# Attention over pooled queries and a multiplicative FFN on one core: each visit's order of work taken from a plan

## The chip, the cores and the metric

The kernel runs on one core of a Trainium2 chip. Its engines have queues of their own: PE multiplies matrices and writes the results into PSUM, DVE and ACT work elementwise and can read PSUM, POOL (GpSimd) works elementwise on SBUF, SP issues DMAs, as ACT and POOL also do. PSUM has eight banks of 128 partitions by 2 KB. The metric is the device time of one execution in microseconds (us); smaller is better.

## The reference

There are 8 batches of 8 heads, with 1152 keys of 64 elements. Neighbouring queries are averaged in pairs, so 576 queries are left for each head. Attention of these, its heads put side by side, is the input x of a feed-forward layer with 4608 tokens:

```python
q_pool = q.reshape(B, H, S // 2, 2, D).mean(axis=3)
scores = scale * np.matmul(q_pool, k.transpose(0, 1, 3, 2))
attn = softmax(scores)                      # over the 1152 keys
x = np.matmul(attn, v)                      # to (4608, 512): tokens by heads * 64
a = x @ w1                                  # (512, 1024)
b = x @ w2                                  # (512, 1024)
out = ((a * b) @ w3) @ w_out                # (1024, 1024), (1024, 512)
```

Nothing stands between w3 and w_out, so the kernel multiplies T = w3 @ w_out once, and then out = (a * b) @ T.

## The kernel before

Everything is unrolled and put on the engines' queues in the order in which the Python code names it; each engine works its queue in that order, and semaphores hold an instruction until its operands are there.

**Attention.** Two heads of one batch are a pair; there are 32 pairs. The loads (`load_kq`, `load_v`) bring K, Q and V in fp32, POOL casts K to fp16 and adds the query pairs (`cast_kq`), and casts V into a tile with a column of constants (`cast_v`), so that the row sums of the softmax come with the product. K and the queries of both heads, 14 blocks of 128 by 128, must be transposed into the tile `kqT`. For pair 0 that is done at the start by `first_loads`, `first_casts` and `first_turn`, for pairs 1 to 7 on PE by `transp_pe` (14 transposes into two PSUM banks, three DVE copies out), and from pair 8 on by a DMA on SP's queue (`transp`).

The scores of all pairs are one long row of columns, cut into 324 slots of 512 columns for each of two heads. `scores(s)` is one slot: matmuls of 64 rows for the two heads at once into a tile of two banks (tag `psc`, three such tiles, so six banks), then one exponential on ACT from it into a ring in SBUF (`ring`). `av_pair` multiplies 128 queries of a pair with V: 18 matmuls into a third of the bank `avb`; five such groups belong to a pair, 160 in all. `av_norm` divides by the row sums on DVE, and x is transposed into `xT`: on PE by `x_turn` and a DVE copy `x_copy` for the pairs below 8 and the last block of every pair, else by a DMA on SP's queue (`x_dma`). `av_step` does these for one group; the turn and copy of a group stand in the step of the next.

**FFN.** `moe_groups` yields the work of a chunk of 512 tokens as groups for PE, each with an evacuation: 8 times a projection with w1 (copied out by DVE) and one with w2 (multiplied with that copy by DVE), then four output groups of eight matmuls against T. `t_groups` yields what T needs: eight times a turn of w3's columns (eight transposes and a DVE copy to `w3T`) and a product of eight matmuls. `fill` takes the next group; it goes to the one bank of tag `mo`, or, if `scored` is true, to a bank of a `psc` tile. w3 comes in four quarters by POOL's queue (`w3_load`).

**The order.** A visit is three score slots and what stands behind them on PE until the next three; there are 108. The loop near the end of the kernel chooses it by counts: `credit` grows with each visit and decides between one AV group and two, and a visit gets two projections (or one group of two units) beside one AV group, and one beside two:

```python
n_av = 0 if not avail else 2 if credit >= (2.6 if two else 1.6) and avail > 1 else 1
credit -= n_av
n_f = 2 if n_av < 2 else 1
```

From visit 3 on T's groups are in the queue (`T_START`), one turn ahead of the products. After the last visit the remaining AV groups alternate with fills, then what is left of the FFN runs without attention. At the end one register is read and a general version of the kernel is skipped.

## Time and profile before

| what | value |
|---|---|
| median of three runs | 424.4 us (424.34 to 425.18) |
| the profiled execution | 425.14 us, its span 423.4 us |
| busy | PE 406.0, ACT 325.3, DVE 202.7, POOL 165.4 us |
| clock granted to PE in the record | 0.999 |
| first score matmul, first exponential | 7.46, 8.11 us |
| visit 18 starts, last visit starts | 69.51, 347.54 us |
| exponentials | 324, 1026 ns each in the record, 950 apart back to back |

A row of the timeline gives a start, the time from the first start to the last end, the engine, the line, what is written from what, the number of instructions (x8) and in brackets how long the engine was idle before and what it waited for. PEld is the loading of weights, which overlaps PE. SPq, ACTq and POOLq stand for the engines' issue of DMAs. Matmuls are pipelined and their ends are modelled, so starts are the surer number.

### The profile page before, as it was taken

The numbers are of one execution on the slowest core, as the hardware profiler recorded it, in microseconds if no ns is written. First come the engines' busy times: TensorE is split into PE (matmuls) and PEld (weight loads), VectorE is DVE, ScalarE is ACT, GpSimd is POOL, SyncE is SP. The second block draws the span as 40 slices with busy tenths as digits, with TensorE's granted clock in tenths as the row PEclk, the third lists the DMA queues.
The fourth block names the chain that finished last, engine by engine and source line by source line (L and its number), as shares of the span: only waits on it lengthen the run. The fifth ranks groups of instructions, "written<-read, shape, count | busy, mean of one in ns | idle before, by whom it ended". The sixth has DMA issues, their size and how long they took to land.

```text
span 423.4 us, 12643 instructions
## 1 busy us (share of the span) xinstructions
PE 406.0 (96%) x5273; PEld 249.6 (59%) x5273; DVE 202.7 (48%) x594; ACT 325.3 (77%) x357; POOL 165.4 (39%) x205
## 2 busy tenths in 40 slices
PE   3889999999999999999999999999999999999995
PEld 1457666666565656665666656666577766444442
DVE  2235554666355544554355534555355536624341
ACT  3968879889999998999889998999999991223231
POOL 4889866370571526323547314351643011000000
PEclk9999999999999999999999999999999999999999
DMA  8999999988494999969999959999994413020203
GB/s 269 256 306 280 289 299 326 261 218 257 144 285 100 264 279 267 258 154 274 299 183 338 268 131 231 254 293 310 280 175 103 58 44 84 12 101 0 99 2 105
DMA packets 90960, 86.34 MB, mean 204 GB/s; under 512 B 59664, under 2 KB 64272, under 8 KB 90896
## 3 DMA queue, kind: packets, MB, share of 16 engines
q1 hardware_dynamic: 81600, 59.52, 57.7%
q0 software_dynamic: 8720, 25.10, 21.1%
q8 instruction: 42, 0.69, 0.7%
q10 hardware_dynamic: 576, 0.85, 0.7%
q14 instruction: 22, 0.18, 0.2%
HBM read 67.11 MB, written 9.44 MB: 181 GB/s over the span
## 4 chain that ended last, share of the span: by engine, by line
PE 89%; DMA 4%; POOL 2%; DVE 2%; ACT 1%; issue 1%; SPq 0%; ACTq 0%; POOLq 0%
PE avb L316 21%; PE psc L291 18%; PE mot L409 16%; PE mo L409 14%; PE mo L447 10%; PE mot L447 5%; PE mo L388 3%; DMA w3c<-in_moe_w_dram 3%; DMA kst<-in_k_dram 1%; ACT ring L296 1%; PE ptk L233 1%; DVE kqT L235 1%; PE mot L388 0%; PE mol L465 0%; PE avb L349 0%
## 5 line engine op out<-in xcount | busy, mean ns | idle before, releaser
L296 ACT ACTIVATE ring<-psc 128x1024 f16<-128x1024 f32 x324 | 307.9, 1026 | 39.8 <-PE psc L291 38.5
L316 PEld LDWEIGHTS <-ring 128*128 128x128 f16 x2880 | 105.1, 98 | 35.3 <-issue 11.2
L316 PE MATMUL avb<-vaug,ring 128*128 128x65 f16 x2880 | 114.1, 193 | 1.5 <-DVE xT L358 1.5
L291 PE MATMUL psc<-kqT 64*128 64x512 f16 (+7 forms) x1152 | 96.0, 290 | 3.2 <-ACT ring L296 1.3
L205 POOL CAST kq<-kst 128x1152 f16<-128x1152 f32 x31 | 35.7, 1151 | 75.2 <-DMA kqT<-kq 46.1
L291 PEld LDWEIGHTS <-kqT 64*128 64x128 f16 x1152 | 45.5, 95 | 29.4 <-issue 6.3
L334 DVE RECIPROCAL rzall<-avb 128x2 f32<-128x2 f32 x160 | 26.3, 164 | 45.4 <-PE avb L316 29.9
L421 POOL DMA_DIRECT2D out_dram<-osb x21 | 11.7, 555 | 87.5 <-DVE rzall L334 87.5
L409 PEld LDWEIGHTS <-w2sb 128*128 128x128 f16 x320 | 28.3, 97 | 26.8 <-issue 2.9
L409 PEld LDWEIGHTS <-w1sb 128*128 128x128 f16 x320 | 28.0, 97 | 27.1 <-issue 3.5
L447 PEld LDWEIGHTS <-gT 128*128 128x128 f16 x280 | 25.4, 98 | 31.2 <-issue 4.0
L447 PE MATMUL mo<-T,gT 128*128 128x512 f16 x184 | 43.6, 380 | 0.0
L409 PE MATMUL mot<-xT,w2sb 128*128 128x512 f16 (+2 forms) x172 | 41.1, 364 | 0.0
L209 POOL TENSOR_TENSOR kq<-qst 128x512 f16<-128x512 f32 x31 | 39.4, 1271 | 1.7 <-DMA qst<-in_q_dram 1.7
L437 DVE TENSOR_TENSOR gT<-mot,asb 128x512 f16<-128x512 f32 x40 | 27.6, 692 | 23.6 <-PE mot L409 23.6
L218 POOL CAST vaug<-vst 128x1152 f16<-128x1152 f32 x32 | 36.6, 1143 | 4.0 <-DMA vst<-in_v_dram 3.7
L409 PE MATMUL mot<-xT,w1sb 128*128 128x512 f16 (+2 forms) x152 | 38.0, 373 | 0.0
L432 ACT COPY asb<-mot 128x512 f32<-128x512 f32 x20 | 11.7, 586 | 32.7 <-PE mot L409 32.7
L434 DVE COPY asb<-mo 128x512 f32<-128x512 f32 x35 | 24.2, 691 | 25.5 <-PE mo L409 25.5
L409 PE MATMUL mo<-xT,w1sb 128*128 128x512 f16 (+2 forms) x168 | 36.1, 344 | 0.0
L457 DVE TENSOR_SCALAR osb<-mo 128x512 f32<-128x512 f32 x23 | 15.9, 692 | 42.3 <-PE mo L447 42.3
L409 PE MATMUL mo<-xT,w2sb 128*128 128x512 f16 (+2 forms) x148 | 33.0, 351 | 0.0
(67 smaller groups left out, 269.9 us busy)
## 6 DMA issues: line engine op xcount, KB each, us to landing
vst<-in_v_dram SPq DMA_DIRECT2D x25, 576.0 KB, 5.0
kst<-in_k_dram SPq DMA_DIRECT2D x23, 576.0 KB, 5.8
qst<-in_q_dram SPq DMA_DIRECT2D x23, 512.0 KB, 6.8
out_dram<-osb POOLq DMA_DIRECT2D x21, 256.0 KB, 5.6
kst<-in_k_dram POOLq DMA_DIRECT2D x8, 576.0 KB, 9.5
qst<-in_q_dram POOLq DMA_DIRECT2D x8, 512.0 KB, 10.6
vst<-in_v_dram POOLq DMA_DIRECT2D x7, 576.0 KB, 6.4
out_dram<-osb SPq DMA_DIRECT2D x9, 256.0 KB, 2.1
```

The costliest lines, as they stand in the source:

```text
L205: nc.gpsimd.tensor_copy(out=kq16[:, 0:NJ].rearrange("p c u d -> p u c d"), in_=kst.rearrange("p u (c d) -> p u c d", d=D))
L209: eng.tensor_tensor(out=kq16[:, NJ:NJ + QM].rearrange("p c u d -> p u c d"), in0=qv[:, :, :, 0], in1=qv[:, :, :, 1], op=ALU.add)
L218: nc.gpsimd.tensor_copy(out=va[:, :, :, 0:D], in_=vs.pop(p).rearrange("p u (c d) -> p u c d", d=D))
L291: nc.tensor.matmul(psc[:, u, f - s * G:f - s * G + ln], kT2[u * 64:u * 64 + 64, jt, :], qpT[u * 64:u * 64 + 64, i0:i0 + ln], start=True, s ...
L296: nc.scalar.activation(out=ring[:, :, r0:r0 + G], in_=psc, func=AF.Exp, bias=0.0, scale=SCALE)
L316: nc.tensor.matmul(avb[:, o + u * E1:o + u * E1 + E1], ring[:, u, c0:c0 + 128], va[:, u, jt, :], start=(jt == 0 and u == 0), stop=(jt == N ...
L334: nc.vector.reciprocal(out=rzall[:, i, :], in_=av[:, :, D:E1].rearrange("p u o -> p (u o)"))
L409: nc.tensor.matmul(pw[:, d0:d0 + n], wt[:, mc, ft * 128:ft * 128 + 128], xT[:, mc, a:a + n], start=(mc == 0 and d0 == 0), stop=(mc == NC - ...
L434: nc.vector.tensor_copy(out=asb, in_=pa)
L437: nc.vector.tensor_tensor(out=gT[:, ft, :], in0=pb, in1=asb, op=ALU.mult)
L447: nc.tensor.matmul(po, gT[:, ft, tt:tt + 128], T16[:, ft, :], start=(ft == 0), stop=(ft == NF - 1))
L457: nc.vector.tensor_scalar_mul(out=osb, in0=po, scalar1=1.0 / (SCL * SCL))
```

## The change

A class `_Plan` keeps a reckoning of times: when PE is at which point, until when ACT and DVE are busy, and when each of the three `psc` tiles, the `mo` bank and the `av` bank come free, with fixed durations for each kind of work. For each visit `_Plan.visit` tries all orders of up to six items out of pair turns (P), up to three AV groups (A) and up to four fills (m for the `mo` bank, s for a scored bank), reckons three score slots behind each order, and takes the one with the least cost: time that PE loses, the distance to a time due (3.12 us for a visit), the wait of the AV bank, less a bonus for AV groups. The emission then follows that string. For the arrival of w3's quarters, of w_out and of pair 2 the plan has fixed times.

T's groups change their order and size: two turns of w3, then four half products of eight matmuls with 256 columns each. The tiles `w3T`, `gT` and `asb` are now taken when a group is emitted, since the queue is read four groups ahead; `near` is set there too.

The first pair: the second half of q is loaded by ACT's queue and the tail of q (64 KB) by SP's, ahead of the rest of K. The cast of K's first three blocks is POOL's, the query sums DVE's. `first_turn` uses one bank for each call: K's first three blocks go through the `mo` bank and are copied by ACT; the four query blocks go through the `av` bank, copied half by DVE and half by ACT; the last query block (`NB - 1`) follows behind slot 0; the other six blocks of K behind slot 2 as before.

In the changed kernel's order the visits 4 to 18 hold, behind their score slots (AV: AV group with its turn of x; half: half product):

```
4  AV, half, AV              9  half, pair 3, AV, half      14  AV, turn, turn, AV
5  AV, half, pair 2, AV      10 turn, AV, turn, half        15  half, pair 5, AV, half
6  half, half, AV            11 AV, half, AV                16  AV, half, AV
7  AV, turn, turn, AV        12 AV, pair 4, AV              17  AV, half, AV
8  half, half, AV            13 half, half, AV              18  projection, projection, AV
```

and before:

```
4  product, AV               9  AV, pair 3, turn, AV        14  AV, turn, AV
5  AV, pair 2, turn, AV      10 product, AV                 15  AV, pair 5, product
6  product, AV               11 turn, product, AV           16  product, AV
7  AV, turn, AV              12 AV, pair 4, turn, AV        17  AV, AV
8  product, AV               13 product, AV                 18  AV, projection, AV
```

The diff, without the lines that only pass on the changed tuples and tiles:

```diff
...
+class _Plan:
+    SWITCH, SLOT, AV, TURN, PAIR, SEEN = 0.09, 0.222, 0.553, 0.055, 0.76, 0.05
+    STEP = {0.5: 0.45, 1: 0.866, 2: 1.73}
+    def __init__(self, t):
+        self.t = t
+        self.act = self.mo = self.av = self.dve = 0.0
+        self.psc = [0.0, 0.0, 0.0]
+        self.k = 0
+        self.row = True
+    def _pe(self, row, free, took):
+        if row != self.row:
+            self.t += self.SWITCH
+            self.row = row
+        self.t = max(self.t, free) + took
+    def _psc(self):
+        self.k += 1
+        return (self.k - 1) % 3
+    def scores(self):
+        b = self._psc()
+        self._pe(True, self.psc[b] + self.SEEN, self.SLOT)
+        self.act = max(self.act, self.t + 0.21) + 0.953
+        self.psc[b] = self.act + 0.07
+    def fill(self, n, at, scored):
+        b = self._psc() if scored else None
+        self._pe(False, max(at, (self.psc[b] if scored else self.mo) + self.SEEN), self.STEP[n])
+        self.dve = max(self.dve, self.t + 0.2) + 0.69
+        if scored:
+            self.psc[b] = self.dve + 0.07
+        else:
+            self.mo = self.dve + 0.07
+    def av_group(self, turns):
+        self._pe(False, self.av + self.SEEN, self.AV + (self.TURN if turns else 0.0))
+        self.dve = max(self.dve, self.t + 0.2) + 0.49 + (0.21 if turns else 0.0)
+        self.av = self.dve + 0.02
+    def pair(self, at):
+        b = self._psc()
+        self._pe(False, max(at, self.psc[b] + self.SEEN), self.PAIR)
+        self.dve = max(self.dve, self.t + 0.1) + 0.9
+        self.psc[b] = self.dve + 0.07
+    def copy(self):
+        p = _Plan(self.t)
+        p.__dict__.update(self.__dict__)
+        p.psc = list(self.psc)
+        return p
+    def visit(self, due, turns, groups, pair_at, eager):
+        best = [None, None]
+        def end(p, seq, work, av):
+            q = p.copy()
+            for _ in range(3):
+                q.scores()
+            lost = q.t - self.t - work - 3 * self.SLOT
+            cost = lost + 0.2 * abs(p.t - due) + 0.3 * max(q.av + self.SEEN - q.t, 0.0)
+            cost -= eager * min(len(turns), 6) * av
+            if best[0] is None or cost < best[0] - 1e-9:
+                best[:] = [cost, seq]
+        def step(p, seq, work, av, f, pr):
+            if pr == len(pair_at):
+                end(p, seq, work, av)
+            if len(seq) > 5 or p.t > due + 0.5:
+                return
+            if pr < len(pair_at):
+                q = p.copy()
+                q.pair(pair_at[pr])
+                step(q, seq + "P", work + self.PAIR, av, f, pr + 1)
+            if av < min(len(turns), 3):
+                q = p.copy()
+                q.av_group(turns[av])
+                step(q, seq + "A", work + self.AV + (self.TURN if turns[av] else 0.0), av + 1, f, pr)
+            if f < min(len(groups), 4):
+                n, at = groups[f]
+                for b in (False, True):
+                    q = p.copy()
+                    q.fill(n, at, b)
+                    step(q, seq + "ms"[b], work + self.STEP[n], av, f + 1, pr)
+        step(self, "", 0.0, 0, 0, 0)
+        return best[1]
...
         qv = q[0, 0:2, 0:QM * 256].rearrange("u (p c) d -> p u (c d)", p=128)
         nc.scalar.dma_start(out=qst[:, 0, :], in_=qv[:, 0, :])
         nc.sync.dma_start(out=kst[:, :, 0:K0 * D], in_=kv[:, :, 0:K0 * D])
-        nc.scalar.dma_start(out=qtl, in_=q[0, 0:2, QM * 256:S].rearrange("u (p t) d -> p u (t d)", t=2))
-        nc.sync.dma_start(out=qst[:, 1, :], in_=qv[:, 1, :])
+        nc.scalar.dma_start(out=qst[:, 1, :], in_=qv[:, 1, :])
+        nc.sync.dma_start(out=qtl, in_=q[0, 0:2, QM * 256:S].rearrange("u (p t) d -> p u (t d)", t=2))
         nc.sync.dma_start(out=kst[:, :, K0 * D:], in_=kv[:, :, K0 * D:])
         kq[0] = (kst, qst, qtl)
...
     def first_casts():
-        kst, qst, qtl = kq.pop(0)
+        kst, qst, qtl = kq[0]
         kv = kst.rearrange("p u (c d) -> p u c d", d=D)
         qv = qst.rearrange("p u (c t d) -> p u c t d", t=2, d=D)
         o = kq16s[0].rearrange("p c u d -> p u c d")
-        nc.vector.tensor_copy(out=o[:, :, 0:K0], in_=kv[:, :, 0:K0])
-        nc.vector.tensor_tensor(out=o[:, 0, NJ:NJ + QM], in0=qv[:, 0, :, 0], in1=qv[:, 0, :, 1], op=ALU.add)
+        nc.gpsimd.tensor_copy(out=o[:, :, 0:K0], in_=kv[:, :, 0:K0])
+        for u in range(2):
+            nc.vector.tensor_tensor(out=o[:, u, NJ:NJ + QM], in0=qv[:, u, :, 0], in1=qv[:, u, :, 1], op=ALU.add)
         nc.gpsimd.tensor_tensor(out=kq16s[0][0:QT, NJ + QM], in0=qtl[:, :, 0:D], in1=qtl[:, :, D:2 * D], op=ALU.add)
-        nc.vector.tensor_tensor(out=o[:, 1, NJ:NJ + QM], in0=qv[:, 1, :, 0], in1=qv[:, 1, :, 1], op=ALU.add)
-        nc.gpsimd.tensor_copy(out=o[:, :, K0:NJ], in_=kv[:, :, K0:])
         kqT = att.tile([128, NB, 128], FP16, tag="kqT", bufs=3)
         pairs[0] = (*kq_views(kqT), kqT)
-    def first_turn(*parts):
+    def rest_casts():
+        kv = kq.pop(0)[0].rearrange("p u (c d) -> p u c d", d=D)
+        nc.gpsimd.tensor_copy(out=kq16s[0].rearrange("p c u d -> p u c d")[:, :, K0:NJ], in_=kv[:, :, K0:])
+    def first_turn(c0, c1, pt, *engs):
         kq16, kqT = kq16s[0], pairs[0][2]
-        pt = ps.tile([128, 512], FP32, tag="mo", bufs=1, name="ptf").bitcast(FP16)
-        o = 0
-        for c0, c1 in parts:
-            for c in range(c0, c1):
-                nc.tensor.transpose(pt[:, o + (c - c0) * 128:o + (c - c0) * 128 + 128],
-                                    kq16[:, c].rearrange("p u d -> p (u d)"), ident16)
-            o += (c1 - c0) * 128
-        o = 0
-        for c0, c1 in parts:
-            nc.vector.tensor_copy(out=kqT[:, c0:c1].rearrange("p c i -> p (c i)"), in_=pt[:, o:o + (c1 - c0) * 128])
-            o += (c1 - c0) * 128
+        for c in range(c0, c1):
+            nc.tensor.transpose(pt[:, (c - c0) * 128:(c - c0) * 128 + 128],
+                                kq16[:, c].rearrange("p u d -> p (u d)"), ident16)
+        w = (c1 - c0) // len(engs)
+        for n, eng in enumerate(engs):
+            o = n * w
+            eng(out=kqT[:, c0 + o:c0 + o + w].rearrange("p c i -> p (c i)"), in_=pt[:, o * 128:(o + w) * 128])
+    def turn_bank():
+        return ps.tile([128, 512], FP32, tag="mo", bufs=1, name="ptf").bitcast(FP16)
...
         w3T = {}
         def turn(ft):
-            w3T[ft] = msb.tile([128, NF, 128], FP16, tag="w3T", bufs=2, name="w3T")
             def go(pt):
+                w3T[ft] = msb.tile([128, NF, 128], FP16, tag="w3T", bufs=2, name="w3T")
                 ph = pt.bitcast(FP16)
                 for a in range(NF):
                     nc.tensor.transpose(ph[:, a * 128:a * 128 + 128],
                                         w3c[ft // 4][:, ft % 4, a * 128:a * 128 + 128], ident16)
-            return 1, go, lambda pt: nc.vector.tensor_copy(out=w3T[ft].rearrange("p a i -> p (a i)"),
-                                                           in_=pt.bitcast(FP16))
-        def mult(ft):
+            return 0.5, go, lambda pt: nc.vector.tensor_copy(out=w3T[ft].rearrange("p a i -> p (a i)"),
+                                                             in_=pt.bitcast(FP16)), W3_AT[ft // 2]
+        def mult(ft, n0):
             def go(pT):
                 for a in range(NF):
-                    nc.tensor.matmul(pT, w3T[ft][:, a, :], wosb[:, a, :], start=(a == 0), stop=(a == NF - 1))
-            return 2, go, lambda pT: nc.vector.tensor_copy(out=T16[:, ft, :], in_=pT)
-        yield turn(0)
-        for ft in range(NF):
-            if ft + 1 < NF:
-                yield turn(ft + 1)
-            yield mult(ft)
+                    nc.tensor.matmul(pT[:, 0:256], w3T[ft][:, a, :], wosb[:, a, n0:n0 + 256],
+                                     start=(a == 0), stop=(a == NF - 1))
+            return 1, go, lambda pT: nc.vector.tensor_copy(out=T16[:, ft, n0:n0 + 256], in_=pT[:, 0:256]), WO_AT
+        for ft in range(0, NF, 2):
+            yield turn(ft)
+            yield turn(ft + 1)
+            for n in range(4):
+                yield mult(ft + n // 2, n % 2 * 256)
...
-    def head():
-        while queue and not ahead:
+    def head(n=1):
+        while queue and len(ahead) < n:
             try:
                 ahead.append(next(queue[0]))
             except StopIteration:
                 queue.pop(0)
-        return ahead[0][0] if ahead else 0
+        return len(ahead)
     def fill(scored=False):
-        n = head()
-        if n:
-            _, go, put = ahead.pop()
-            pt = bank(scored) if put else None
-            go(pt)
-            if put:
-                put(pt)
-        return n
+        if not head():
+            return False
+        n, go, put, at = ahead.pop(0)
+        if not tail[0]:
+            plan.fill(n, at, scored)
+        pt = bank(scored) if put else None
+        go(pt)
+        if put:
+            put(pt)
+        return True
...
     first_casts()
+    rest_casts()
...
+    plan = _Plan(7.0)
+    PACE = 3.12
+    W3_AT, WO_AT, KQ_AT = (17.5, 28.0, 35.0, 44.0), 20.5, {2: 24.5}
...
-    seen = -1
-    credit = 0.0
-    vis = 0
-    while vis < NVIS or avn[0] < NU:
+    seen, due, started = -1, 0.0, False
+    for vis in range(NVIS):
         if vis == T_START:
             queue.append(t_groups())
+        due = max(due + PACE, plan.t + 2.6)
+        for s in range(vis * VS, vis * VS + VS):
+            pn = (s * G + G - 1) // FLAT
+            if pn != seen:
+                seen = pn
+                if pn == 0:
+                    first_turn(0, K0, turn_bank(), nc.scalar.copy)
+                    first_turn(NJ, NJ + QM, avb.bitcast(FP16), nc.vector.tensor_copy, nc.scalar.copy)
+                if NPE <= pn + 1 < NP:
+                    transp(pn + 1)
+                if 0 < pn < NP - 2:
+                    prepare(pn + 2)
+                elif pn + 2 == NP:
+                    cast_v(NP - 1)
+            scores(s)
+            plan.scores()
+            if s == 0:
+                first_turn(NB - 1, NB, turn_bank(), nc.vector.tensor_copy)
+        if vis == 0:
+            first_turn(K0, NJ, turn_bank(), nc.vector.tensor_copy)
+            prepare(2)
+        avail = NT5 * sum(1 for e in pair_end if e < vis) - avn[0]
+        turn = [p for p in range(1, NPE) if (p * FLAT // G) // VS - 1 == vis]
+        while ready:
+            started = True
+            queue.append(moe_groups(ready.pop(0)))
+        head(4)
+        for what in plan.visit(due, [on_pe(avn[0] + j - 1) for j in range(avail)], [(g[0], g[3]) for g in ahead],
+                               [KQ_AT.get(p, 0.0) for p in turn], 0.05 if started else 0.1):
+            if what == "P":
+                plan.pair(KQ_AT.get(turn[0], 0.0))
+                transp_pe(turn.pop(0))
+            elif what == "A":
+                av_step()
+                plan.av_group(on_pe(avn[0] - 2))
+            else:
+                fill(what == "s")
+    fill(True)
+    while avn[0] < NU:
+        av_step()
         while ready:
             queue.append(moe_groups(ready.pop(0)))
-        if vis < NVIS:
...
-        avail = NT5 * sum(1 for e in pair_end if e < vis) - avn[0]
-        turn = [p for p in range(1, NPE) if (p * FLAT // G) // VS - 1 == vis]
-        if vis >= NVIS:
-            fill(True)
-            while avn[0] < NU:
-                av_step()
-                fill(True)
-            break
-        credit = min(credit + NU / (NVIS - 5.0), float(avail)) if avail else 0.0
-        two = head() == 2
-        n_av = 0 if not avail else 2 if credit >= (2.6 if two else 1.6) and avail > 1 else 1
-        credit -= n_av
-        n_f = 2 if n_av < 2 else 1
-        if n_f == 2 and not turn:
-            if not two:
-                fill()
-            fill(not two)
-            if n_av:
-                av_step()
-        else:
-            if n_av:
-                av_step()
-            for p in turn:
-                transp_pe(p)
-            fill()
-            if n_av > 1:
-                av_step()
-        vis += 1
+        fill(True)
     tail[0] = True
     x_turn(NU - 1)
     x_copy(NU - 1)
```

## The prediction

> **What bounds the kernel now.** First the page's busy times and its slices, then the chain of what ended last.
>
> ```profile
> PE 406.0 (96%) x5273; PEld 249.6 (59%) x5273; DVE 202.7 (48%) x594; ACT 325.3 (77%) x357; POOL 165.4 (39%) x205
> ...
> PEclk9999999999999999999999999999999999999999
> ...
> PE 89%; DMA 4%; POOL 2%; DVE 2%; ACT 1%; issue 1%; SPq 0%; ACTq 0%; POOLq 0%
> ```
>
> PE ends the kernel, and the change leaves its work as it is: the same 324 score slots, 160 AV groups, 144 projections, 36 output groups, 64 transposes of w3, all in order on one queue. The time can then move only by what PE waits, so I need a list of waits. Busy time does not give it (matmul ends are modelled), but starts do: the distance from the first matmul of a group to the first of the next, less the shortest such distance of that kind, is the wait. The timeline of PE, undisturbed:
>
> ```profile
> 28.31 0.71 PE L316 MATMUL avb<-vaug,ring 128*128 128x65 f16 x18
> 28.86 0.22 PE L349 MATMUL avb<-ident,xbt 128*128 128x128 f16 x1
> 29.01 0.83 PE L291 MATMUL psc<-kqT 64*128 64x512 f16 x10
> 29.76 1.90 PE L388 MATMUL mo<-wosb,w3T 128*128 128x512 f16 x8
> 31.50 0.71 PE L316 MATMUL avb<-vaug,ring 128*128 128x65 f16 x18
> ```
>
> So an AV group is 0.55 us (28.86 - 28.31), its x transpose 0.15 with the change to scores, three slots 0.75, a T product 1.74. From the start of the w3 transposes at 33.59 to the AV at 34.47, below, 0.45 is work and the rest a wait; a pair turned on PE is 0.78, a projection 0.86 to 0.87, an output group 1.73. Measured against these, PE waits until 7.46 for its first score, then 13.3 us in visits 0 to 17 (up to 69.51), 6.1 us in visits 18 to 106, and next to nothing after the last score slots at 347.54. What can be won lies before 70 us.
>
> **Where the early waits are.** Visits 0 to 4 hold 7.3 us: ACT has nine exponentials back to back from 8.11 to 16.47 and PE has nothing else to do. The change brings no other work there. Then:
>
> ```profile
> 14.69 1.65 PE L233 MATMUL ptk<-ident,kq 128*128 128x128 f16 x14 [0.31 <-ACT ring L296]
> ...
> 24.89 0.95 PE L233 MATMUL ptk<-ident,kq 128*128 128x128 f16 x14
> 27.85 0.62 PE L379 MATMUL mo<-ident,w3c 128*128 128x128 f16 x8 [2.00 <-DMA w3c<-in_moe_w_dram]
> ...
> 34.47 0.72 PE L316 MATMUL avb<-vaug,ring 128*128 128x65 f16 x18 [0.27 <-DVE xT L358]
> ...
> 68.82 0.71 PE L316 MATMUL avb<-vaug,ring 128*128 128x65 f16 x18 [0.72 <-DVE xT L358]
> ```
>
> Visit 5 turns pair 2 at 24.89 and then stands 2.2 us for the second quarter of w3 (issued 16.88, landed 27.80). POOL's last cast for that pair ends at the same time:
>
> ```profile
> 24.39 0.45 POOL L211 TENSOR_TENSOR kq<-qtl 64x128 f16<-64x128 f32 x1
> ```
>
> Visits 6 to 17 hold 3.7 us in small waits: an AV or T product behind a w3 transpose (0.43, 0.36, 0.44 in visits 7, 11, 14), a second AV straight after the first (0.9, visit 17), T products behind the copies of pair and w3T (0.17, 0.17, 0.09), a pair waiting for its scored bank (0.20, 0.17), a late score slot (0.34, visit 15), and 0.4 in crumbs.
>
> **The change part by part.** The visits' contents of the changed kernel can be read from its instruction order.
>
> *The w3 turn of visit 5.* It moves to visit 7 as a pair of transposes; visit 5 becomes AV, half product, pair 2, AV. Visit 5 starts at 23.36 now; visit 4 gets some 0.4 shorter, its exponentials end near 22.7 and so free the last bank of visit 5 at about 22.9; with a slot, AV and half product behind that PE reaches the pair at about 24.7. But the cast ends at 24.84, so it starts at 24.9; then 0.78 + 0.55 + 0.15: visit 6 starts at 26.5 instead of 29.01, with 0.2 us more done (one AV more, one turn fewer). 2.7 us won. Its cover is the arrival of pair 2: each us by which that is later or earlier costs or gives one. The loads behind it keep their order on POOL's queue, with one cast of 384 columns added ahead of a cast that waits for its data until 7.68 anyway; I take 24.84, and 0.5 us either way for the range. The second quarter of w3 is then used near 31, the third (landed 34.8) near 40, the fourth (42.8) near 53. wosb, for which a POOL load waits until 20.38, is used at about 20.8.
>
> *Visits 6 to 17.* Two transposes together (0.9) cover the norm and the copy that the next AV waits for (0.69 after the matmuls), so the waits of 7, 11 and 14 go; the AV pair of visit 17 gets a half product between (0.86 against 0.93). A pair no longer shares a visit with a w3 turn, so its three copies (1.22 on DVE) do not stand ahead of w3T's. What is late next: three exponentials take 2.85, and these visits now hold 2.9 to 3.3 of PE work, so score slots will now and then wait 0.1; a pair right after an AV still waits 0.2. I leave 0.9 of 3.7: 2.8 won, between 1.8 and 3.3. DVE's eight more T copies are half as wide.
>
> *Half products.* 128 matmuls of 256 columns instead of 64 of 512. The nearest row is a projection cut in eight pieces: 0.87 against 0.86 in four, 2.5 ns a piece, so 64 more cost 0.16. The upper end, 0.5 us, is a weight load (98 ns) showing at times behind a 107 ns matmul.
>
> *The first pair.* K's first cast goes from DVE to POOL (about 0.1 slower), so the q sums don't wait behind it; the second half of q goes on ACT's queue, with 64 KB instead of 256 KB ahead of K's rest on SP's; q is copied in halves by DVE and ACT, and 128 columns of 640 wait until after slot 0. Both halves lie in one bank, and the instruction order shows ACT's copy waiting for DVE's, as here:
>
> ```profile
> 413.62 0.42 DVE L453 TENSOR_SCALAR osb<-mot 128x256 f32<-128x256 f32 x1 [0.96 <-PE mot L447]
> 414.08 0.38 ACT L454 ACTIVATE osb<-mot 128x256 f32<-128x256 f32 x1 [2.46 <-DVE osb L453]
> ```
>
> The halves follow each other, 414.08 after 413.62 + 0.42. So 0.25 + 0.38 take the place of 0.76, and the score starts at about 7.3, 0.2 earlier (ends: 0.5 earlier, 0.5 later if the q transfer is). Worth nothing: visit 5 waits for pair 2's cast either way. By the Trainium skill, PSUM — Partial Sum Buffer, "PSUM bank collisions raise a hardware error", ScalarE and VectorE must not touch one bank and the same partitions at once, two reads included; with that the halves can't overlap and the sum has nothing for it, without it 0.25 would be won ahead of the same cast. The pair of rows above agrees.
>
> *Visits 18 to 106.* Their work is the same by kind. 35 visits of two AVs and one projection (36 before) keep their waits of about 0.1. One visit holds two AVs alone (2.1 us of PE work, and ACT needs 2.85) and one a single output group (2.6): 0.8 and 0.25 lost. The waits before two pair turns (0.2 each) go, and some crumbs with the visits of three projections. Net 0.4 lost, between 0.6 won and 1.5 lost.
>
> *Sum.* -2.7 - 2.8 + 0.16 + 0.4 = -4.9 us. The profiled execution took 425.14 us (span 423.4 and 1.7 around), so 420.2 for one like it; it stands 0.74 above the median of 424.4, and 424.4 - 4.9 = **419.5 us**. Taking all good ends gives -2.7 - 0.5 - 3.3 - 0.6 = -7.1, all bad ones -2.2 - 1.8 + 0.5 + 1.5 = -2.0; these coming together is unlikely.
>
> **Rivals.**
> *The early visits gain little more than visit 5.* PE runs at half pace at first: pair 1's 14 transposes take 1.65 at 14.69, pair 2's 0.95 at 24.89, though the clock line shows 9 all along. The first eight w3 transposes take 0.83, the next eight 0.68, so the change comes near 19.3. Should it come one like stretch later, some 3.4 us of work takes twice its time, 1.7 lost; with 1.0 more of small waits kept, 422. For it: the start of the sequence is rearranged. Against it: visits 2 and 3 do the same work. By the Trainium skill, TensorE: Matmul & The Clock Gate, "What's actually happening", the clock opens after a busy window of about 3.4 us that runs free of the kernel; by that rule one window late is 1.7, as the rows give; no run here shows it late. Chance 0.2.
> *Slower: a pair's DMA transpose lands late.* From pair 8 on, kqT is turned by DMA from SP's queue, in order behind the transposes of x, which wait for AV norms.
>
> ```profile
> 131.33 1.19 SPq L326 DMA_TRANSPOSE xT<-xb  x1
> 132.62 1.54 SPq L225 DMA_TRANSPOSE kqT<-kq  x1
> ```
>
> This one is used at 140.1, 7.5 later. An x transpose stands directly ahead of 15 of 24 now, of 18 in the changed order. Landing took 4.0 to 12.0 us: a late issue with a long landing stalls all scores by up to 4.5. Two such lose the whole gain, three give 428; it decides from a landing over 7.2. Against it: every one that was issued this late landed in 4.0 to 6.2, the long ones were issued early. Chance 0.07.
> *The order is not what pays.* The visits with little PE work grow ACT gaps, and what is won early is given back later: 424.4. Chance 0.04; the counts above speak against it.
> *More than forecast.* Pair 2 arrives 0.5 earlier and the late visits gain 0.6: 418. Chance 0.08.
>
> **Numbers.** The forecast has the remaining 0.61, with a range of its own of 418.3 to 420.9. The 80% range adds most of the first rival and part of the good one: 418.0 to 422.5. This kernel's measurement tells 0.2% (0.85 us) from no change: faster 0.89 (forecast, better, first rival), same 0.04, slower 0.07.
>
> **What will show it.** Visit 18's first score near 65.5 (69.51 - 5.5 + 1.3 for work done sooner), the last three slots near 346.4 with 3.8 us less work behind them; no wait on w3c over 0.5; pair 2 still at 24.9; ACT's copy of q behind DVE's. Wrong would be: pair 2 later than 25.5, PE waiting on kqT from DMA, waits of visits 18 to 106 over 8 us in sum.

## The result, and the profile after

The changed kernel takes 423.3 us (median; 422.5 to 423.86), the kernel before, on the same chip in the same session, 425.18 us (424.34 to 427.45): a ratio of 0.9946, 95% interval 0.9925 to 0.9967. A second session gave 423.1 against 425.47 us, 0.9941 (0.9919 to 0.9963). By the ratio the change makes the kernel faster by 0.54%, 2.3 us (1.9 by the two medians); the prediction had 4.9. The time lies 3.8 above the forecast of 419.5 us. Of these, 0.8 come from the start of the sum: the kernel before had a median of 424.4 in its first three runs and of 425.2 to 425.9 later.

The page of the changed kernel, busy times, clock line and the chain by engine, shows PE bounding as before:

```profile
PE 406.1 (97%) x5337; PEld 252.5 (60%) x5337; DVE 205.9 (49%) x602; ACT 325.8 (77%) x358; POOL 165.7 (39%) x206
...
PEclk9999999999999999999999999999999999999998
...
PE 92%; DMA 3%; ACT 2%; DVE 1%; issue 0%; ACTq 0%; DVEq 0%
```

PE has 64 matmuls more, from the half products. The profiled execution took 422.73 us, with a span of 420.74, against 425.14 and 423.37 before. In its timeline around pair 2, start first, then duration:

```profile
24.11 1.04 PE L484 MATMUL mo<-wosb,w3T 128*128 128x256 f16 x8
24.98 0.94 PE L328 MATMUL ptk<-ident,kq 128*128 128x128 f16 x14
25.77 0.71 PE L413 MATMUL avb<-vaug,ring 128*128 128x65 f16 x18
26.32 0.22 PE L446 MATMUL avb<-ident,xbt 128*128 128x128 f16 x1
26.47 0.61 PE L388 MATMUL psc<-kqT 64*128 64x512 f16 x6
27.25 0.39 PE L388 MATMUL psc<-kqT 64*128 64x128 f16 x4 [0.17 <-DVE kqT L330]
...
31.54 0.61 PE L475 MATMUL mot<-ident,w3c 128*128 128x128 f16 x8
31.98 0.61 PE L475 MATMUL mo<-ident,w3c 128*128 128x128 f16 x8
32.42 0.71 PE L413 MATMUL avb<-vaug,ring 128*128 128x65 f16 x18
```

The second quarter of w3 is used at 31.54 without a wait, visit 6 starts at 26.47 instead of 29.01, and the AV group behind the pair of turns follows after 0.44. But the score slot at 27.25 now waits for a copy of pair 2.

The waits of PE, summed as in the prediction (the distance from a group's start to the next, less the shortest such distance of its kind: AV 0.55, projection 0.86, and so on), say where the time went. "Rest" is the span less all columns before it: work, and the end behind the last visit. Each row is one execution.

| execution | first score | visits 0-4 | 5 | 6-17 | 18-32 | 33-106 | rest | span |
|---|---|---|---|---|---|---|---|---|
| before | 7.46 | 7.26 | 2.39 | 3.68 | 1.32 | 4.80 | 396.46 | 423.37 |
| changed | 6.79 | 7.29 | 0.07 | 1.88 | 1.12 | 6.47 | 397.12 | 420.74 |
| changed, second session | 7.03 | 7.07 | 0.07 | 1.89 | 1.11 | 5.53 | 396.83 | 419.53 |

So 2.3 is won in visit 5, 1.8 in visits 6 to 17 and 0.2 in 18 to 32; 0.7 to 1.7 is given back in visits 33 to 106, and the rest grows by 0.4 to 0.7. The first score comes 0.4 to 0.7 earlier, but visit 3 does not (16.28 and 16.52 against 16.27), so this is no gain (see the first pair, below). These two executions lie 0.6 and 1.6 us below the medians of their kernel's runs, so the last half microsecond of the account is not to be trusted; visits 5 to 32 agree to 0.01.

The giving back has two places. In visit 62 two AV groups stand alone, and the second waits for the normalisation of the first:

```profile
205.06 0.83 PE L388 MATMUL psc<-kqT 64*128 64x384 f16 x10
205.82 0.72 PE L413 MATMUL avb<-vaug,ring 128*128 128x65 f16 x18
207.13 0.72 PE L413 MATMUL avb<-vaug,ring 128*128 128x65 f16 x18 [0.59 <-DVE xbt L439]
```

1.31 lie between the two groups instead of 0.55; visit 63 loses another 0.20, visit 75 (behind a lone output group) 0.32. In visit 81 something else happens:

```profile
256.94 7.50 SPq L423 DMA_TRANSPOSE xT<-xb  x2
...
264.53 2.44 SPq L320 DMA_TRANSPOSE kqT<-kq  x1
266.81 0.29 DVE L439 TENSOR_TENSOR xb<-avb,rzall 128x128 f16<-128x128 f32 x1 [0.95 <-DMA xT<-xb]
...
267.29 0.71 PE L413 MATMUL avb<-vaug,ring 128*128 128x65 f16 x18 [0.77 <-DVE xT L457]
```

DVE may not write the attention output `xb` of a new pair: its buffer, one of two, is still being read by a DMA transpose. The x copy for the next AV group stands behind that write on DVE, so PE waits 0.94. The kernel before has such a wait of DVE too (1.58 us at 272.97), but PE loses nothing by it.

### The profile page after: what moved, and what is told of

The parts are those of the page before. It is cut to its first block, busy times and chain, and to the rows that moved or that the text cites. A ratio compares the mean times of both kernels' runs of the same rounds, so it can differ in the third digit from the quotient of the medians.

```text
span 420.7 us, 12784 instructions
## 1 busy us (share of the span) xinstructions
PE 406.1 (97%) x5337; PEld 252.5 (60%) x5337; DVE 205.9 (49%) x602; ACT 325.8 (77%) x358; POOL 165.7 (39%) x206
## 4 chain that ended last, share of the span: by engine, by line
PE 92%; DMA 3%; ACT 2%; DVE 1%; issue 0%; ACTq 0%; DVEq 0%
PE avb L413 22%; PE psc L388 20%; PE mot L506 15%; PE mo L506 14%; PE mo L550 10%; PE mot L550 5%; PE mo L484 3%; DMA xT<-xb 2%; PE ptk L328 2%; ACT ring L393 1%; DMA qst<-in_q_dram 1%; PE mot L484 1%; PE mot L475 1%; DVE kqT L330 1%; PE mo L475 0%; PE mol L568 0%
## 5 line engine op out<-in xcount | busy, mean ns | idle before, releaser
L413 PEld LDWEIGHTS <-ring 128*128 128x128 f16 x2880 | 103.5, 98 | 33.4 <-issue 11.2
L550 PE MATMUL mo<-T,gT 128*128 128x512 f16 x192 | 45.5, 380 | 0.0
L506 PEld LDWEIGHTS <-w2sb 128*128 128x128 f16 x320 | 28.5, 97 | 26.5 <-issue 2.3
L506 PE MATMUL mot<-xT,w2sb 128*128 128x512 f16 (+2 forms) x164 | 40.1, 369 | 0.0
L506 PE MATMUL mo<-xT,w1sb 128*128 128x512 f16 (+2 forms) x172 | 39.2, 355 | 0.0
L535 DVE COPY asb<-mo 128x512 f32<-128x512 f32 x38 | 26.3, 692 | 23.5 <-PE mo L506 23.5
L506 PE MATMUL mot<-xT,w1sb 128*128 128x512 f16 (+2 forms) x148 | 34.9, 362 | 0.0
L506 PE MATMUL mo<-xT,w2sb 128*128 128x512 f16 (+2 forms) x156 | 34.0, 346 | 0.0
```

Of the source, the lines that this page charges most:

```text
L413: nc.tensor.matmul(avb[:, o + u * E1:o + u * E1 + E1], ring[:, u, c0:c0 + 128], va[:, u, jt, :], start=(jt == 0 and u == 0), stop=(jt == N ...
L506: nc.tensor.matmul(pw[:, d0:d0 + n], wt[:, mc, ft * 128:ft * 128 + 128], xT[:, mc, a:a + n], start=(mc == 0 and d0 == 0), stop=(mc == NC - ...
L535: nc.vector.tensor_copy(out=t["a"], in_=pa)
L550: nc.tensor.matmul(po, t["g"][:, ft, tt:tt + 128], T16[:, ft, :], start=(ft == 0), stop=(ft == NF - 1))
```

## Experiments

All kernels compute the whole reference. The kernel before, beside them on the same chip, had medians of 425.77, 425.88 and 425.47 us in the three sessions, in the order told here. The first session has the first four kernels, the second the next four, the third the last three.

| kernel | median us | ratio to before (95%) | 5 | 6-17 | 33-106 |
|---|---|---|---|---|---|
| late_counts | 422.98 | 0.992 (0.9889 to 0.995) | 0.07 | 1.89 | 5.01 |
| all_counts | 426.99 | 1.001 (0.998 to 1.004) | 0.44 | 3.65 | 8.50 |
| old_first | 423.07 | 0.9932 (0.9896 to 0.9968) | 0.08 | 2.22 | 5.83 |
| xb3 | 422.43 | 0.9908 (0.9876 to 0.994) | 0.07 | 1.89 | 5.69 |
| late_counts_xb3 | 422.55 | 0.9914 (0.9882 to 0.9945) | 1.47 | 1.88 | 6.02 |
| all_counts_xb3 | 423.64 | 0.9953 (0.993 to 0.9977) | 0.19 | 3.65 | 4.94 |
| held3_xb3 | 422.03 | 0.9902 (0.9863 to 0.9941) | 0.07 | 1.89 | 5.66 |
| t_old | 425.2 | 0.9989 (0.996 to 1.0019) | 0.18 | 4.25 | 6.67 |
| after2 (the change again) | 423.1 | 0.9941 (0.9919 to 0.9963) | 0.07 | 1.89 | 5.53 |
| whole | 425.24 | 0.9994 (0.9965 to 1.0022) | 0.18 | 2.98 | 8.49 |
| before_xb3 | 425.19 | 0.9988 (0.9961 to 1.0014) | 4.42 | 4.23 | 4.81 |

The last three columns are waits of PE by visits in the one profiled execution, in us.

### The plan, late and early

late_counts uses the old counting rule from visit 33 on, all_counts in every visit (`vis < 0`). Both keep the new groups of T and the new first pair.

```diff
-        for what in plan.visit(due, ...):
+        if vis < 33:
+            order = plan.visit(due, ...)
+        else:
+            n_av = 0 if not avail else 2 if credit >= (2.6 if two else 1.6) and avail > 1 else 1
+            ...
+        for what in order:
```

> Up to visit 32 as in the changed kernel, from visit 33 on the order by counts of the kernel before. PE's waits in visits 33 to 106 were 4.8 us before and are 6.5 in the changed kernel. Theory A (the plan's late orders cost this: a visit of two AVs alone, one of a single output group, visits of three projections): they fall to 4.8 to 5.1, and the time is 1.4 to 1.7 us below the changed kernel's, ratio to before about 0.991. Theory B (the late waits come with everything running some 4.8 us sooner, so that DMAs land late): they stay above 6 and the ratio stays at 0.994 to 0.995.

> No plan: every visit by the counts of the kernel before; T in pairs of turns and half products and the new first pair are kept. Theory A (the regrouping of T wins the early time, the plan little of it): visit 5 has no wait on w3, waits after the start up to visit 17 are 9 to 10.5 us (9.2 in the changed kernel, 13.3 before), those after it about 6 as before; ratio 0.990 to 0.993, at least as fast as the changed kernel. Theory B (the early time is won by the planned orders): waits up to visit 17 stay above 11.5 and the ratio is 0.996 or more.

With the old rule from visit 33 on, visits 33 to 106 wait 5.01: 0.5 less than the change's second execution, 1.5 less than its first. Part of the first difference is thus not the plan's. The time of late_counts can't be told from that of the change. Without the plan anywhere, visit 5 is still won (0.44): the new groups of T do that alone. Visits 6 to 17 are back at 3.65, so with the new groups the plan is worth 1.8 there; with the old groups it is worth nothing there (4.25 in t_old, below, against 3.68 before). By the same account the waits from the first score to the end of visit 17 come to about 12 us, and the ratio is 1.001, so of the two expectations theory B holds, but for visit 5. The late visits lost 3.7 more than before; in the timeline of all_counts:

```profile
273.62 0.29 DVE L439 TENSOR_TENSOR xb<-avb,rzall 128x128 f16<-128x128 f32 x1 [3.51 <-DMA xT<-xb]
...
274.10 0.71 PE L413 MATMUL avb<-vaug,ring 128*128 128x65 f16 x18 [1.53 <-DVE xT L457]
```

The wait for the buffer again, 3.51 on DVE here; PE lost 1.70 in front of this AV group and another 1.6 in the visit behind it, where it ran at half clock (last section).

### The third buffer

xb3, late_counts_xb3, all_counts_xb3 and before_xb3 are the changed kernel, the two above and the kernel before, each with one edit more:

```diff
-                xb5[p] = att.tile([128, QM, 2, D], FP16, tag="xb5", bufs=2, name="xb5")
+                xb5[p] = att.tile([128, QM, 2, D], FP16, tag="xb5", bufs=3, name="xb5")
```

> The changed kernel with three instead of two buffers for x on its way to SP's transpose (xb5). Theory A (visit 81's 0.94 us is DVE's write waiting for a buffer that SP's late transpose still reads): that wait goes, waits of visits 33 to 106 fall from 6.5 to 5.4 to 5.7, time 0.7 to 1.0 below. Theory B (the transpose itself is late and something else waits for it): the same time is lost at the next projection or score slot of that pair, and the sum stays.

> The changed kernel with the old counting rule from visit 33 on and a third buffer for the attention output that the DMA turns. Theory A (two separate losses behind visit 33: the plan's two poor visits, some 1.2 us, and a normalisation that waits until the DMA turn ahead has read its buffer, 0.4 to 0.9 us): PE's waits of visits 33 to 106 fall to 4.2 to 4.9 us (5.01 with the old rule alone, 5.69 with the third buffer alone, 6.47 in the changed kernel, 4.80 before), the wait of the normalisation on the DMA is gone from DVE, and the time is 0.988 to 0.991 of the kernel before. Rival B (the late loss is one thing that both edits remove, so together they give no more than either): waits 5.0 to 5.7 us and 0.991 to 0.993.

> No plan in any visit (the old counting rule throughout), T as pairs of turns with half products and the new first pair kept, and a third buffer for the attention output that the DMA turns. Theory A (without the plan the early waits of visits 6 to 17 stay, and the loss of visits 33 to 106 was the buffer alone): visit 5 waits 0.4 us, visits 6 to 17 some 3.6 us as before, visits 33 to 106 4.6 to 5.2 instead of 8.5, and the time is 0.993 to 0.996 of the kernel before: what the new groups of T win alone. Rival B (the old rule with the new groups of T is bad for the late visits for its own order): visits 33 to 106 stay over 6.5 us and the time within 0.998 to 1.002.

> The kernel before with a third buffer for the attention output that the DMA turns, and nothing else. Theory A (the normalisation waits for that buffer in the kernel before as well, but PE feels only 0.4 us of it, in visit 79): visits 33 to 106 wait 4.3 to 4.6 us against 4.80, no wait of the normalisation on the DMA is left, and the time is 0.997 to 1.000 of the kernel before. Rival B (the third buffer's 0.0038 in the changed kernel came from elsewhere, as from other addresses or other DMAs): the time is 0.994 to 0.997 here too, with visits 33 to 106 unchanged.

DVE waits for the DMA of `xb` in six of the eight profiles with two buffers (0.6 to 3.5 us) and in none of the five with three. all_counts falls from 1.001 to 0.9953, as expected, with 4.94 instead of 8.50. xb3 gives 0.9908, its interval overlapping that of the change, so a gain by the third buffer under the plan is not shown; the second execution of the change, with two buffers, had no wait for it either.

Two expectations failed. late_counts_xb3 should have waited 4.2 to 4.9 behind visit 33 and waited 6.02. Two events are in it that its sister does not have: 0.72 in visit 95 in the middle of a projection, where the record names no cause ("issue"), and 0.38 in visit 93. Without them it is 4.92, hardly better than late_counts: the profiles fit two separate losses, that of the plan's late orders and the buffer's, the second not in every execution; the times do not show them apart. The same profile shows an event that the prediction had priced:

```profile
25.79 1.26 POOL L304 TENSOR_TENSOR kq<-qst 128x512 f16<-128x512 f32 x1 [1.55 <-DMA qst<-in_q_dram]
27.02 0.44 POOL L306 TENSOR_TENSOR kq<-qtl 64x128 f16<-64x128 f32 x1
...
27.52 0.95 PE L328 MATMUL ptk<-ident,kq 128*128 128x128 f16 x14 [1.23 <-POOL kq L306]
```

Pair 2's queries landed late, its cast ended 2.7 later than in the changed kernel's profile, and visit 5 waited 1.47.

before_xb3 should have shown 4.3 to 4.6 behind visit 33. The wait of DVE is gone, but PE's waits stay at 4.81, and so does the 0.4 of visit 79 that had been put down to it (a score slot behind an exponential). So in the kernel before the short buffer costs nothing.

### The projections held back

held3_xb3 lets the FFN start a chunk when three AV groups instead of five are still ahead of it, so that visit 62 gets a projection between its two AV groups (third buffer as above).

```diff
-    HELD = 5
+    HELD = 3
```

> The plan in all visits, with three AV groups held back ahead of the FFN instead of five, and a third buffer as in the run before. The order changes in visit 62, which then holds a projection between its two AV groups. Theory A (the 0.96 us of visits 62 and 63 is an AV group that waits for the normalisation of the one straight ahead of it): this wait goes, visits 33 to 106 wait 4.5 to 5.0 us against 5.69 with the third buffer alone, 0.989 to 0.991 of the kernel before. Rival B (the projections were held back because their x would not be there yet): a projection waits for the DMA of x by 0.5 us or more at the chunk borders, and visits 33 to 106 stay at 5.5 to 7.

The wait of 0.76 in visit 62 is gone and that of 0.20 in visit 63 smaller, as theory A has it. The sum is still 5.66, as with five (5.69). The waits of 0.26 and 0.38 in visits 54 and 75 stand in xb3 as well (0.26 and 0.33); new are 0.21 and 0.30 in visits 87 and 100 and 0.1 to 0.2 more in each of visits 78, 80, 82, 91 and 106. Theory A was right on the place and wrong on the sum. The time, 0.9902, is the lowest of all kernels, with an interval that overlaps that of xb3.

### The groups of T

t_old has T's old groups under the plan (one turn, then a whole product). whole has pairs of turns, but whole products (its edit, with the lines of the 512-column product left out):

```diff
...
-            for n in range(4):
-                yield mult(ft + n // 2, n % 2 * 256)
+            for n in range(2):
+                yield mult(ft + n)
```

> The changed kernel with T's old groups: one turn of w3 ahead of each whole product of 512 columns; the plan and the new first pair stay. Theory A (the plan alone moves the second turn out of visit 5, since it knows when the second quarter of w3 lands; the regrouping matters for the small waits only): visit 5 waits under 0.4 us, visits 6 to 17 wait 2.2 to 3.7 us against 1.88, and visits 18 to 106 7.0 to 8.0, so that the time is 0.995 to 1.000 of the kernel before. Rival B (the regrouping is what moves the turn of w3 behind visit 5): PE stands over 1.5 us for w3's second quarter in visit 5 or 6, and the time is 0.999 to 1.004. Half products cost 0.2 us in the sum by distance of starts (0.88 a half against 1.724 a whole), and this goes in both theories.

> The changed kernel with two turns of w3 ahead of two whole products instead of four half products; plan and first pair stay. Theory A (the pairs of turns cover the copies that an AV group waits for, 1.3 us in three visits of the kernel with the old groups of T; the halves fill the visits, worth about 1 us, at 0.2 to 0.3 us of PE time): no wait of 0.4 us behind a turn of w3 is left, visits 6 to 17 wait 2.3 to 3.2 us against 1.88 and 4.25, and the time is 0.995 to 0.999 of the kernel before. Rival B (the halves are what the plan needs): visits 6 to 17 stay at 3.8 us or more, and the time is 0.998 to 1.002. Rival C (the halves are worth nothing): 2.0 us or less, and 0.992 to 0.995.

Visit 5 is won in both (0.18). So either part, plan or groups, moves the use of w3's second quarter behind its arrival; the prediction credited the groups. Visits 6 to 17 are 4.25 with single turns, 2.98 with pairs, 1.88 with half products. With single turns the AV group behind each still waits, here in t_old (0.88 from the start of the turn, 0.45 of it work):

```profile
32.54 0.61 PE L475 MATMUL mo<-ident,w3c 128*128 128x128 f16 x8
...
33.42 0.71 PE L413 MATMUL avb<-vaug,ring 128*128 128x65 f16 x18 [0.27 <-DVE xT L457]
```

Three such waits of 0.43 are the 1.27 between 4.25 and 2.98, so the pairs do what was said; the halves bring another 1.1, most of it in score slots (in whole six of them wait 0.25 to 0.46, in the change two wait 0.33). t_old's 6 to 17 lie outside the 2.2 to 3.7 expected. In whole, 1.95 of the 8.49 in the late visits is the buffer (visit 54), 0.70 an "issue" wait as above (visit 96); the 5.84 left are near the 5.53 of the change. Its time, 0.9994, lies above the 0.995 to 0.999 expected: of the 2.1 us between its median and the change's, visits 6 to 17 explain 1.1. The rest fits its late visits, but whole was not run with a third buffer.

### The first pair

old_first has the loads, casts and the turn of the first pair as in the kernel before.

```diff
...
-                    first_turn(0, K0, turn_bank(), nc.scalar.copy)
-                    first_turn(NJ, NJ + QM, avb.bitcast(FP16), nc.vector.tensor_copy, nc.scalar.copy)
+                    first_turn((0, K0), (NJ, NB))
...
```

> The changed kernel with the loads, casts and turns of the first pair as before. Theory A (the earlier first score is given back at once: slot 1 waits for the late query block, slot 3 for the rest of K): first score at 7.4 to 7.5 instead of 6.8, slot 3 and visit 3 start where they do in the changed kernel (10.4 and 16.3), time within 0.3 us of it. Theory B (the 0.67 us is kept): visit 3 and the end come 0.5 to 0.7 later.

The first score is 0.81 later (7.60 against 6.79), but visit 3 starts at 16.40 against 16.28; the ratio, 0.9932, can't be told from that of the change. Nothing was won. In the changed kernel's timeline:

```profile
6.04 0.29 DVE L373 COPY kqT<-avb 128x256 f16<-128x256 f16 x1 [0.70 <-PE avb L368]
6.37 0.37 ACT L373 COPY kqT<-avb 128x256 f16<-128x256 f16 x1 [0.56 <-DVE kqT L373]
6.79 0.61 PE L388 MATMUL psc<-kqT 64*128 64x512 f16 x2 [0.79 <-ACT kqT L373]
...
7.94 1.03 PE L388 MATMUL psc<-kqT 64*128 64x64 f16 x8 [0.32 <-DVE kqT L373]
...
10.38 1.30 PE L388 MATMUL psc<-kqT 64*128 64x320 f16 x10 [0.38 <-DVE kqT L373]
```

Slot 1 waits at 7.94 for the query block that was put off, and a later slot at 10.38 for K's rest (10.34 before). What the first slot gains ends there: from the first score to visit 3 the changed kernel takes 9.49 us, old_first 8.80 and the kernel before 8.81.

### The change again

> The changed kernel once more, beside the same runs of the kernel before as the next two, for what one execution can tell. Theory A (its waits are set by its order, the waits for a DMA and the start vary from one execution to the next): visit 62 waits 0.7 to 0.8 us again and visits 6 to 17 wait 1.8 to 1.95; the normalisation's wait for the DMA turn of the output ahead of visit 81 lies anywhere from 0 to 1.5 us on PE, and start and visits 0 to 4 together between 14.0 and 15.3 us; the time is 0.993 to 0.997 of the kernel before. Rival B (that wait is fixed by the order as well): 0.9 to 1.0 us in visit 81 again.

Visit 62 waits 0.76 again, visits 6 to 17 wait 1.89, start and visits 0 to 4 take 14.10. In visit 81 nothing waits this time, although SP issues the two transposes of `xb` at 256.96 as against 256.94 in the first execution: the issue is the same, so the wait depends on when they land. Rival B falls.

## Why the prediction was right or wrong

**Bound and direction: right.** PE bounds before and after, and the gain is in waits. In the changed kernel's profile none of the three signs of a wrong forecast came: pair 2 is not later than 25.5, PE waits for no kqT from DMA, the waits of visits 18 to 106 are 7.6 us, under 8. They were set too wide: the forecast was missed without any of them. Visit 6 starts on time (26.47 against 26.5), visit 18 at 66.21 against 65.5, the last three slots at 348.28 (347.36 in the second session) against 346.4.

**Visit 5: the number right, its cover in part by luck.** Pair 2 starts at 24.98 (forecast 24.9), visit 6 at 26.47 (26.5). But POOL's cast does not hold it:

```profile
24.32 0.44 POOL L306 TENSOR_TENSOR kq<-qtl 64x128 f16<-64x128 f32 x1
```

The cast ends at 24.76, and PE starts the pair 0.87 after the half product ahead of it (24.11 to 24.98), the shortest such distance. PE came 0.3 later than the 24.7 reckoned, and so the two ends met by chance. That a late pair 2 would cost shows in late_counts_xb3, where the cast ends 2.7 later: visit 5 waits 1.47 there, the rest being covered, since visit 5 itself starts 1.1 later (23.87). Of the 2.7 forecast, 2.39 was there to win as a wait, so some 0.4 is work moved between visits; and the plan alone would have won it as well.

**Visits 6 to 17: the step that failed.** "I leave 0.9 of 3.7: 2.8 won, between 1.8 and 3.3": 1.88 are left, 1.8 won, the bad end. The named waits of 7, 11 and 14 and of visit 17 went, the pairs alone taking 1.27. Mis-sized is "what is late next", which had 0.9 for all: score slots wait 0.33 in visits 6 and 13 each (the first for copies of pair 2), the turns of w3 wait 0.12 and 0.18 behind an AV group, pair 4 waits 0.16, and 0.8 are crumbs. Where a score slot waits for an exponential, the table's 950 ns from one to the next is too long: the nine from 8.11 take 8.36 us, 0.92 apart, and the plan reckons with 0.953.

**Visits 18 to 106: sized right by its order, one wait not seen.** "Net 0.4 lost, between 0.6 won and 1.5 lost" was 0.5 lost in the second execution and 1.47 in the first; the difference is 0.94 of the buffer. The 0.8 for two AV groups alone is the 0.76 of visit 62. The slower rival looked at SP's queue, but at the wrong user: no kqT was late; the DMA transpose of x, in the same queue behind loads and before kqT, held a buffer that DVE writes.

**Half products: 0.16 forecast.** Two halves in a row start 0.88 apart (33.91 to 34.79) against 0.87 for half of a whole: 16 of them make about 0.16. The rest of the account grew by 0.4 to 0.7, though; t_old and whole, with whole products, show 0.3 to 0.4 of it too, so the halves do not explain it all. The new first pair is a likely part: it adds 0.68 between the first score and visit 3 (9.49 against 8.81), with one turn and its slot more there, and the account counts part of this as work. How much was not tried.

**First pair: the value right, the cause wrong.** The first score came at 6.66 to 7.35 in the ten profiles of kernels with the new first pair (7.3 forecast), and it is worth nothing. But not because visit 5 waits for pair 2: the gain ends in visits 0 to 3. Visit 5 starts 0.6 earlier (22.73 against 23.36), but that is won in visits 3 and 4, where 0.25 us of work less is done and less is waited. ACT's copy starts at 6.37, after DVE's 6.04 + 0.29, like the pair of rows in the trace of before. The Trainium skill, PSUM — Partial Sum Buffer, "PSUM bank collisions raise a hardware error", has it that ScalarE and VectorE must not touch one bank and the same partitions at once; the trace agrees.

**The rivals.** The first came nearest by what it wins (2.4), by a mechanism that did not happen in this profile: pair 1 takes 1.65 and pair 2 0.94 after as before, and of the first two turns of w3 the second is fast already. In other profiles that change of pace comes later; the second turn first in the changed kernel, then in late_counts, which has the same order up to there:

```profile
19.07 0.64 PE L475 MATMUL mo<-ident,w3c 128*128 128x128 f16 x8
```

```profile
19.63 1.06 PE L475 MATMUL mo<-ident,w3c 128*128 128x128 f16 x8
```

From visit 3 to visit 5 late_counts takes 6.91 us, the changed kernel 6.45 and 6.23 in its two executions. The second turn takes 1.06 in five of the 13 profiles, old_first with its old first pair among them, so this looks like scatter of about half a microsecond and not like the doing of the change. Of "what is won early is given back later" a part came true: 0.7 to 1.7 of the 4.3 won up to visit 32.

**The sum.** For one execution like the profiled one 420.2 was forecast, and it took 422.73, 2.5 more: 1.0 from visits 6 to 17, 1.1 from the late visits, 0.4 from visit 5 and 0.5 from the rest, less 0.6 at the first score; 0.2 lies outside the span. (The 0.6 and the 0.5 belong together in part, as the 0.68 up to visit 3 shows.) The bad ends of all terms together would have made 2.0 won and 422.4 us; with the 0.8 by which the kernel before was slower later, 423.2. So what put 423.3 outside 418.0 to 422.5 was the two mis-sized terms and a base taken from three runs, after the judgement that the bad ends "coming together is unlikely".

## What to carry to other kernels

Where a queue is re-ordered, look at every buffer that a slow DMA still reads, not only at what the DMA delivers: here a third buffer of `xb` is the cheapest edit seen: all_counts goes from 1.001 to 0.9953 by it. With the plan (0.9908) a gain is likely and not shown, and in the kernel before (0.9988) it gained and cost nothing that shows. When waits are removed, size what comes next from the work in each visit against the engine beside it instead of leaving a round remainder: two score slots alone made 0.66 of the 1.88 left in visits 6 to 17. And read one-execution profiles with their scatter: repeat the profile before a wait of half a microsecond on a DMA is called the order's doing.

## What was not expected of the hardware

A wait of PE can cost more than its length, since the clock may fall behind it. In the profile of before_xb3, whose order up to there is that of the kernel before, w3's second quarter is late and PE stands 2.85 us by the record instead of 2.00:

```profile
24.57 0.95 PE L233 MATMUL ptk<-ident,kq 128*128 128x128 f16 x14 [0.26 <-POOL kq L211]
28.38 1.03 PE L379 MATMUL mo<-ident,w3c 128*128 128x128 f16 x8 [2.85 <-DMA w3c<-in_moe_w_dram]
29.20 1.20 PE L316 MATMUL avb<-vaug,ring 128*128 128x65 f16 x18
```

The eight transposes take 1.03 instead of 0.62 and the AV group 1.20 instead of 0.71. The table of windows of the same profile (window, length, busy time of PE, PEld, DVE, ACT and POOL with instructions, granted clock, DMA share, GB/s) and then that of all_counts behind its wait of 1.70 show the clock granted:

```profile
26.00:28.00 2.00, 0.00 (x0) 0.00 (x0) 0.78 (x3) 0.06 (x1) 1.94 (x3) 1.00 1.03 403
28.00:30.00 2.00, 1.62 (x23) 1.63 (x24) 0.55 (x1) 0.00 (x0) 2.00 (x3) 0.54 0.88 210
```

```profile
274.00:276.00 2.00, 1.89 (x37) 1.42 (x37) 1.61 (x5) 0.77 (x1) 0.47 (x1) 0.97 1.11 187
276.00:278.00 2.00, 2.00 (x18) 1.13 (x16) 0.46 (x2) 2.00 (x3) 2.00 (x3) 0.50 0.98 376
```

The same table with narrower windows has half clock from 28.18 to 31.59 and from 275.87 to 279.27, 3.4 us each time. So visit 5 lost 4.42 in before_xb3 instead of 2.39, and all_counts lost 1.6 in the visit behind its wait. Length alone does not decide: behind the wait of 2.2 us in the kernel before, and of 1.95 in whole, the clock stayed. By the Trainium skill, TensorE: Matmul & The Clock Gate, "What's actually happening", the clock goes cold after an idle window of about 3.4 us, and the windows run free of the kernel. None of these waits filled 3.4 us (the longest, by starts, is the 3.0 of before_xb3), so at that figure the trace differs; that it depends on where the wait lies would agree with free-running windows, but is not shown.

The times of the runs fit this in part. Of 67 runs of the kernel before, beside the experiments, 34 have a mean granted clock of at least 0.997 and take 425.1 us (median; the highest 426.1); 33 have at most 0.996 and take 427.1. But six of these 33 take 425.2 or less, the fastest of all (423.86) among them, so a low mean does not tell where the clock fell: in before_xb3's profile a second stretch at half clock lies at 14.5 to 17.9 us, where pair 1 takes the same 1.65 as in the profile of the kernel before. Of 21 runs of the changed kernel none is below 0.996, and they end between 421.5 and 423.9, with a median of 423.1. Against the 34 runs at 0.997 or more the change thus wins 2.0 us, and what the ratio shows beyond that would be the clock that no longer falls. That it falls behind visit 5's wait is shown in one execution, and argued for the others.
